# Two attentions on one core: half pairs of exponentials for VectorE, memory and B's first segment asked sooner

## The chip, the cores and the metric

One core of a Trainium2 chip. Its engines run their own instruction streams beside each other: TensorE (PE, with the weight loads PEld shown apart), VectorE (DVE), ScalarE (ACT), GpSimd (POOL) and SyncE (SP), which here issues nearly all DMAs. The metric is the device time of one execution in microseconds (us); lower is better.

## The reference

Two independent attentions over 2048 tokens of width 576 with 32 heads of 18, all float32; their outputs are concatenated.

```python
# A: one key and one value head for all query heads
q = heads(x @ wq); k = x @ wk; v = x @ wv
p = softmax(einsum("bhqd,bkd->bhqk", q, k) * Dh ** -0.5)
a = merge(einsum("bhqk,bkd->bhqd", p, v)) @ wo
# B: four segments of 512, causal inside a segment, and a running memory
for s in range(4):
    logits = einsum("bhqd,bhkd->bhqk", qs, ks) * scale + mask
    a_dot = einsum("bhqk,bhkd->bhqd", softmax(logits), vs)
    a_mem = einsum("bhld,bhde->bhle", phi(qs), M) / (einsum("bhld,bhd->bhl", phi(qs), z)[..., None] + 1e-6)
    o = g * a_mem + (1.0 - g) * a_dot
    M = M + einsum("bhld,bhle->bhde", phi(ks), vs); z = z + einsum("bhld->bhd", phi(ks))
b = merge(o) @ wo
```

## The kernel before, in words

The first part (L156 to L606, up to about 290 us) projects q, k and v of A and B, splits them into float32r parts, stores them to DRAM, and sums B's memory. The attention stage follows, and its order on PE, ACT and DVE is written out by hand (L1086).

Its work is cut into blocks. A block of A, `("A", c, hg)`, is one chunk of 512 queries and four heads (two "pairs" of heads, `pr` 0 and 1) against 16 key tiles `kt` of 128: 32 items. A block of B, `("B", s, hg)`, is one segment and four heads against three key tiles: 6 items. There are 32 of each. `after` (L869) says behind which block of A each pair of B blocks runs; the pair shares one stack of operands. `its` lists the items, `turns` cuts each block into turns of three items, with one turn of two (the last one) in a block of A: 11 turns of A, 2 of B. `prods` does the same for the products, with its short turn at another place (`cut`).

The loop at L1110 makes one turn k:

- `scores` (L905) for the items of turn k: two matmuls for a pair into `E`, a PSUM tile of two banks, one bank per head; there are three such tiles. Then exponentials on ACT into `P`. The second item of a turn (`copied`) is first copied by DVE from `E` to `W` in SBUF, so that its PSUM tile comes free before ACT has reached it; ACT does it last.
- One step of B's memory (`ask_memory`, L809, from turn `ASK` on and only where the turn is all of A), or, when that has ended, one step of an output projection (`run_fill`, L856; 60 steps a projection, eight projections in all, two of which are done in the tail).
- One step of `slow`: pairs named in `BY_DVE` have their exponential computed by VectorE from bit operations and a polynomial (`exponentials`, L890, seven operations, into the tile `PD`). The first reads PSUM in the pair's own turn, the six others follow one a turn. Their products come late in the block, at the place that `LATE` gives.
- `products` (L949) for turn k-2: P times V into `O`. With the last products of a block, DVE copies `O` out and SP stores it.
- `due`: steps put down for later, which normalize finished heads (`finish`).

Operands come by DMA on SP in program order: `load_stackB` (L688) loads queries, bounds and keys of eight heads of B into `stB`, of which there are two buffers (16 issues a stack); `load_stackA` does the same for A; `load_vseg` loads a segment's values (one buffer); `load_qf` and `ask_memory` load what the memory step needs, for two segments, into `o` and `woA`. `prefetch` asks for the stack after the one in use. L997 to L1003 set the order at the start.

The tail, from L1141, ends the projection that has begun and does the last two with PE alone (L1163).

Of the kernel before, what the change touches and what calls it, by code (L numbers as in the profile page):

```python
# [8 lines left out]
F32 = mybir.dt.float32  # L9
# [3 lines left out]
U32 = mybir.dt.uint32  # L13
AF = mybir.ActivationFunctionType
# [14 lines left out]
SCALE = DH ** -0.5  # L29
# [3 lines left out]
PBUFS = 9  # L33
# [18 lines left out]
POLY = [1.0925606709321247, 32.334180715292455, 88.7610992882796, 4291.093056129828]  # L52
MANTISSA, ONE_BITS, EXPONENT = 0x7FFFFF, 0x3F800000, 0xFF800000

BY_DVE = ((0, 1),)
LATE = (12,)
QALL = [(slice(0, 36, 2), 0), (slice(1, 36, 2), 1), (slice(36, 54), 0)]
CA = 618
MZ = 126 + 32

LATE_ASK, ASK = (1, 2), 20


def below(rows, r0):
# [10 lines left out]
def attention_pair_kernel(ctx, tc, a_xT, a_w, a_wo, b_xT, b_w, b_wo, b_beta, ident_d, hmask_d, bmask_d, cmask_d, sel_d, zmask_d, selx_d, sely_d, out):  # L75
    nc = tc.nc
# [727 lines left out]
    def load_qf(s):  # L804
        qfs[s] = pa.tile([128, 5, C], F32, name="o", bufs=2)
        nc.sync.dma_start(qfs[s][:126, :4], qfB[s][:126, :4])
        nc.sync.dma_start(qfs[s][: RT[4], 4], qfB[s][: RT[4], 4])
# [47 lines left out]

    def run_fill():  # L856

        while fill:
            key, steps = fill[0]
            if next(steps, None) is not None:  # L860
                begun.add(key)
                filled[0] += 1
                return
            fill.pop(0)


    blocksA = [("A", c, hg) for c in range(NCH) for hg in range(8)]
    blocksB = [[("B", s, 2 * h8), ("B", s, 2 * h8 + 1)] for s in range(NSEG) for h8 in range(4)]
    after = [0, 0, 1, 1, 2, 3, 3, 4, 8, 9, 10, 12, 16, 17, 18, 20]  # L869
    blocks = []  # L870
    for n, b in enumerate(blocksA):
        blocks.append(b)
# [14 lines left out]

    slow, now = [], [0]

    def exponentials(p, e):  # L890

        y, u, w = p.bitcast(U32), pp.tile([128, 2, 512], F32, name="n", bufs=1), pp.tile([128, 2, 512], F32, name="q", bufs=1)
        v, stt = nc.vector, nc.vector.scalar_tensor_tensor
        v.tensor_scalar(y, e, EXP_A, EXP_B, op0=ALU.mult, op1=ALU.add)
        steps = [
            lambda: v.tensor_scalar(u.bitcast(U32), y, MANTISSA, ONE_BITS, op0=ALU.bitwise_and, op1=ALU.bitwise_or),
            lambda: v.tensor_scalar(w.bitcast(U32), y, EXPONENT, None, op0=ALU.bitwise_and),
            lambda: stt(p, u, POLY[0], u, op0=ALU.add, op1=ALU.mult),
            lambda: stt(p, p, POLY[1], u, op0=ALU.add, op1=ALU.mult),
            lambda: stt(p, p, POLY[2], p, op0=ALU.add, op1=ALU.mult),  # L900
            lambda: stt(p, p, POLY[3], w, op0=ALU.add, op1=ALU.mult),
        ]
        slow.extend((now[0] + 2 + i, p, step) for i, step in enumerate(steps))

    def scores(it, pr, copied):  # L905

        ab, c, hg, kt = it
        st = stacks[ab, c, hg // 2]
        h = 2 * (hg % 2) + pr
        e = psE.tile([128, 2, 512], F32, name="E")  # L910
        dve = ab == "A" and (kt, pr) in BY_DVE
        p = pp.tile([128, 2, 512], F32, name="PD" if dve else "P", bufs=1 if dve else PBUFS)
        state[it, pr] = p
        n = 512 if ab == "A" else 512 - 128 * kt if kt < 2 else 384
        if ab == "A":
            for j, r0 in enumerate(HALF):
                rows = slice(r0, r0 + KR)
                nc.tensor.matmul(e[:, j], kstA[rows, 128 * kt : 128 * kt + 128], st[rows, h, :], start=True, stop=True)  # L918
            if (kt, pr) in BY_DVE:
                exponentials(p, e)  # L920
                return lambda: None
        else:
            for k, c0 in BKEYS[kt]:
                ks = slice(128 * k, 128 * k + 128)
                for j, r0 in enumerate(HALF):
                    rows = slice(r0, r0 + KR)
                    nc.tensor.matmul(  # L927
                        e[:, j, c0 : c0 + 512 - 128 * k], st[rows, 4 + h, ks], st[rows, h, 128 * k :], start=True, stop=True
                    )
        src = e  # L930
        if copied:
            src = pp.tile([128, 2, 512], F32, name="W", bufs=2)
            nc.vector.tensor_copy(src[:, :, :n], e[:, :, :n])  # L933

        def exponential():
            nc.scalar.activation(p[:, :, :n], src[:, :, :n], AF.Exp, scale=SCALE)  # L936
            if ab == "B":

                m = len(BKEYS[kt])
                diag = p.rearrange("p a (b t) -> p a b t", t=256)[:, :, 0:m, 0:128]  # L940
                nc.gpsimd.affine_select(  # L941
                    diag, diag, pattern=[[0, 2], [0, m], [1, 128]], base=0, channel_multiplier=-1, compare_op=ALU.is_ge, fill=0.0
                )

        return exponential
# [3 lines left out]
    def products(b, m, hf):  # L949


        ab, c, hg = b
        if m == hf == 0:
            acc[0] = psO.tile([128, C], F32, name="O")
        o = acc[0]
        last = (NKT - 1 if ab == "A" else 2) == m
        for j in range(4):
            kt = turn_of[j // 2][m] if ab == "A" else m
            p = state[b + (kt,), j // 2]
            assert all(x[1] is not p for x in slow)  # L960
            k, p0, q0, n = (kt, 256 * hf, 256 * hf, 256) if ab == "A" else BHALF[kt][hf]
            if ab == "A":
                v = VA[:, VW * kt : VW * kt + 32]
            else:
                v = vseg[c][:, k, VW * (4 * hg + j) : VW * (4 * hg + j) + 32]
            nc.tensor.matmul(  # L966
                o[32 * j : 32 * j + 32, q0 : q0 + n],
                v,
                p[:, j % 2, p0 : p0 + n],
                start=m == hf == 0,  # L970
                stop=last and hf == 1,
            )
        if last and hf:
            osb = pa.tile([128, C], F32, name="oe", bufs=4)
            nc.vector.tensor_copy(osb, o)  # L975
            od = oA if ab == "A" else oB
            nc.sync.dma_start(od[c][4 * hg : 4 * hg + 4].rearrange("h r t -> (h r) t"), osb)
            return hg
        return None
# [12 lines left out]
    def prefetch(ab, upto):  # L992
        for k in keys[ab][:upto]:
            if k not in stacks:
                stacks[k] = (load_stackA if ab == "A" else load_stackB)(*k[1:])

    prefetch("B", 1)  # L997
    load_vseg(0)
    prefetch("B", 2)
    load_qf(1)  # L1000
    memory = ask_memory()
    next(memory)
    prefetch("A", 2)  # L1003
    FILL = 60
    later, weighed, loaded, summing = [], {}, [0], set()
# [80 lines left out]
    with tc.manual_schedule(engines={ENG.PE, ENG.Activation, ENG.DVE}):  # L1086
# [3 lines left out]
        for n, b in enumerate(blocks):  # L1090
            ms = [m for m in range(len(its)) if block_of[m] == n]
            items = [(m, k) for m in ms for k in range(2)]
            for out_, cut in ((turns, len(items) // 3), (prods, len(items) // 3 - 2)):
                at_ = split(len(items), cut)
                out_ += [items[a:z] for a, z in zip(at_, at_[1:])]
        at(ASK + 4, 0, lambda: True, lambda k: load_qf(2))
# [13 lines left out]
        for k in range(len(turns) + 2):  # L1110
            now[0] = k
            exps = [scores(its[n], pr, i == 1) for i, (n, pr) in enumerate(turns[k])] if k < len(turns) else []
            for i in (0, 2, 1) if len(exps) == 3 else range(len(exps)):
                exps[i]()
            if memory is None:
                run_fill()
            elif k >= ASK and all(its[n][0] == "A" for n, pr in turns[k]) and next(memory, None) is None:
                memory = None

            ends = k > 1 and any(hf and its[n][3] == (NKT - 1 if its[n][0] == "A" else 2) for n, hf in prods[k - 2])  # L1120
            if slow and (slow[0][0] <= k or not ends):
                slow.pop(0)[2]()
            for n, hf in prods[k - 2] if k > 1 else []:
                ab, c = its[n][:2]
                hg = products(its[n][:3], its[n][3], hf)
                if hg in (6, 7):
                    finish(k, ab, c, hg)
                if hg == 7 and ab == "B" and c + 1 < NSEG:
                    load_vseg(c + 1)
            due(k)  # L1130
            if k == len(turns):
                halve_w(0)
            for n, pr in turns[k] if k < len(turns) else []:
                it = its[n]
                ab = it[0]
                if pr == 0:
                    prefetch(ab, keys[ab].index((ab, it[1], it[2] // 2)) + 2)
                    if it in (("A", 0, 2, 8), ("A", 0, 5, 8)):
                        load_wo(*(("B", b_wo) if it[2] == 2 else ("A", a_wo)))

        while fill and fill[0][0] in begun:  # L1141
            due(k, 4)
            run_fill()
            if filled[0] % FILL == 0:
                fill.pop(0)
            k += 1

        rows = [key for key, steps in fill] + [blocks[-1][:2]]
# [113 lines left out]
```

## Time and profile before

| | us |
|---|---|
| median of 3 runs | 1418.96 (1418.83 to 1419.97) |
| profiled execution | 1422.47, its span 1420.7 |
| PE busy | 1404.0 (99%) |
| ACT busy | 1205.4 (85%) |
| DVE busy | 964.4 (68%) |
| POOL busy | 244.6 (17%) |
| ACT, exponentials from PSUM (L936, P<-E) | 800 of them, 780.8 busy |
| ACT, exponentials from SBUF (L936, P<-W) | 384 of them, 426.3 busy |
| DVE, copies W (L933) | 384 of them, 461.2 busy |

Busy times are the union of an engine's instructions. Instructions of one engine overlap in the records, so the time that one costs is read from its start to the start of the next, not from its length. A busy PE is not a PE at its limit. In the timeline rows a bracket gives the idle time before a row and what ended it; SPq rows are issues of DMAs, with no landing time.

### The profile page before, as it was taken

To read this page: it belongs to the slowest core of one execution; us is meant where nothing else is said; L and a number is where in the kernel's file an instruction comes from. 1 tells how busy PE (TensorE), PEld (TensorE's weight loads), DVE (VectorE), ACT (ScalarE), POOL (GpSimd) and SP (SyncE) were. 2 spreads that over 40 slices of the span, in tenths; PEclk is the share of its full clock that TensorE was granted. 3 is DMA by queue.
4 is the path that set the end of the run, shared out by engine and by line. 5 is a ranking of instruction groups with operands and counts; after the bars stand their busy time and mean duration, and the time that the engine had idled before them with its cause. 6 is when DMAs were issued, how large, how long until landed. Compare 5 with 4: busy or idle time off the path is not lost.

```text
span 1420.7 us, 39951 instructions
## 1 busy us (share of the span) xinstructions
PE 1404.0 (99%) x17132; PEld 843.3 (59%) x17132; DVE 964.4 (68%) x1157; ACT 1205.4 (85%) x1447; POOL 244.6 (17%) x326
## 2 busy tenths in 40 slices
PE   9999999999999999999999999999999999999998
PEld 6788888745555555555555555555555555555558
DVE  6656456456677767776766777666767766777663
ACT  4543434479999999999999999999999999999991
POOL 2431000003313213221110160131011400100002
PEclk9999999999999999999999999999999999999999
DMA  9766546557564535332312543232104221110013
GB/s 283 253 216 188 166 146 214 174 171 214 156 214 159 165 120 166 91 109 77 110 58 70 166 128 92 62 107 80 51 34 132 67 76 44 60 45 18 9 59 112
DMA packets 90720, 172.63 MB, mean 122 GB/s; under 512 B 14576, under 2 KB 22889, under 8 KB 90110
## 3 DMA queue, kind: packets, MB, share of 16 engines
q1 hardware_dynamic: 84122, 160.01, 36.0%
q0 software_dynamic: 1664, 4.78, 1.3%
q10 hardware_dynamic: 4752, 5.24, 1.1%
q8 instruction: 135, 2.21, 0.7%
q14 instruction: 47, 0.39, 0.1%
HBM read 99.32 MB, written 70.67 MB: 120 GB/s over the span
## 4 chain that ended last, share of the span: by engine, by line
PE 68%; ACT 7%; issue 2%; DMA 1%; DVE 1%; SPq 0%; ACTq 0%; DVEq 0%
PE O L966 31%; PE E L918 20%; PE F L773 11%; ACT P L936 7%; PE E L927 3%; PE E L1163 2%; PE F L829 1%; DMA stB<-qB 0%; DVE W L933 0%; PE F L1163 0%; PE O L1163 0%; DMA oA<-oe 0%; DMA stB<-kB 0%; DMA sm<-oA 0%; SPq L696 0%
## 5 line engine op out<-in xcount | busy, mean ns | idle before, releaser
L936 ACT ACTIVATE P<-E 128x1024 f32<-128x1024 f32 (+1 forms) x800 | 780.8, 1059 | 12.7 <-PE E L918 12.3
L933 DVE COPY W<-E 128x1024 f32<-128x1024 f32 (+1 forms) x384 | 461.2, 1201 | 248.8 <-PE E L918 189.2
L966 PE MATMUL O<-P,VA 128*32 128x256 f32 x7936 | 508.8, 380 | 0.0
L936 ACT ACTIVATE P<-W 128x1024 f32<-128x1024 f32 (+1 forms) x384 | 426.3, 1110 | 3.4 <-DVE W L933 3.2
L966 PEld LDWEIGHTS O<-P,VA 128*32 128x32 f32 x7936 | 262.2, 110 | 147.6 <-issue 6.6
L918 PE MATMUL E<-stA,kstA 56*128 56x512 f32 x1920 | 329.4, 439 | 1.8 <-DVE W L933 1.1
L918 PEld LDWEIGHTS E<-stA,kstA 56*128 56x128 f32 x1920 | 154.7, 184 | 178.2 <-ACT P L936 113.7
L941 POOL TENSOR_SCALAR_AFFINE_SELECT P<-P 128x256 f32<-128x256 f32 (+1 forms) x192 | 95.0, 495 | 480.3 <-ACT P L936 446.9
L761 POOL TENSOR_TENSOR o<-o,rb 126x512 f32<-126x512 f32 (+1 forms) x55 | 79.9, 1468 | 408.9 <-DMA o<-oA 146.0
L773 PE MATMUL F<-woB,o 126*32 126x192 f32 (+1 forms) x1920 | 127.4, 338 | 0.3 <-DVE osb L797 0.3
L966 PE MATMUL O<-P,vseg 128*32 128x256 f32 (+2 forms) x1536 | 81.8, 344 | 0.8 <-issue 0.8
L773 PEld LDWEIGHTS F<-woB,o 126*32 126x32 f32 (+1 forms) x1920 | 38.2, 108 | 70.6 <-issue 63.6
L975 DVE COPY oe<-O 128x512 f32<-128x512 f32 x64 | 44.3, 692 | 41.8 <-PE O L966 41.0
L252 PE MATMUL pj<-xh,wBl 128*126 128x512 f32 x180 | 72.4, 403 | 0.0
L252 PE MATMUL pj<-xh,wBh 128*126 128x512 f32 x180 | 71.9, 400 | 0.0
L121 ACT CAST qp<-pj 126x512 fp32r<-126x512 f32 (+1 forms) x54 | 31.0, 585 | 46.1 <-DVE kmB L450 32.4
L966 PEld LDWEIGHTS O<-P,vseg 128*32 128x32 f32 x1536 | 49.1, 109 | 25.4 <-issue 2.9
L773 PE MATMUL F<-woA,o 126*32 126x192 f32 (+1 forms) x960 | 63.9, 338 | 0.0
L927 PE MATMUL E<-stB 56*128 56x256 f32 (+3 forms) x512 | 61.3, 347 | 1.4 <-ACT P L936 0.9
L122 DVE TENSOR_TENSOR qp<-pj,qp 126x512 fp32r<-126x512 f32 (+1 forms) x54 | 36.7, 685 | 35.6 <-ACT qp L121 35.3
L252 PE MATMUL pj<-xl,wBh 128*126 128x512 f32 x144 | 57.3, 399 | 0.0
L927 PEld LDWEIGHTS E<-stB 56*128 56x128 f32 x512 | 38.6, 185 | 31.1 <-ACT P L936 20.8
(194 smaller groups left out, 1387.8 us busy)
## 6 DMA issues: line engine op xcount, KB each, us to landing
stB<-kB SPq DMA_DIRECT2D x96, 144.0 KB
stB<-qB SPq DMA_DIRECT2D x32, 288.0 KB
stA<-qA SPq DMA_DIRECT2D x30, 288.0 KB
oA<-oe SPq DMA_DIRECT2D x32, 256.0 KB
oB<-oe SPq DMA_DIRECT2D x32, 256.0 KB
qA<-qp SPq DMA_DIRECT2D x16, 504.0 KB
kB<-qp SPq DMA_DIRECT2D x16, 504.0 KB
qB<-qp SPq DMA_DIRECT2D x16, 504.0 KB
```

The costliest lines, as they stand in the source:

```text
L121: hold(nc.scalar.copy(qp[:R, 0, :n], src))
L122: hold(nc.vector.tensor_tensor(qp[:R, 1, :n], src, qp[:R, 0, :n].bitcast(F32), op=ALU.subtract))
L252: nc.tensor.matmul(dst, w[:, c0 : c0 + M], x, start=i == 0, stop=i == len(ops) - 1)
L761: return lambda: tc.keep_in_program_order(nc.gpsimd.tensor_tensor(dst, a, b, op=op))
L773: nc.tensor.matmul(dst[32 * j : 32 * j + 32], parts[ab, c][: RT[t], t, r0 : r0 + 32], wo[ab][: RT[t], t, c0 : c0 + n], start=start, stop=stop,
L918: nc.tensor.matmul(e[:, j], kstA[rows, 128 * kt : 128 * kt + 128], st[rows, h, :], start=True, stop=True)
L927: nc.tensor.matmul(e[:, j, c0 : c0 + 512 - 128 * k], st[rows, 4 + h, ks], st[rows, h, 128 * k :], start=True, stop=True)
L933: nc.vector.tensor_copy(src[:, :, :n], e[:, :, :n])
L936: nc.scalar.activation(p[:, :, :n], src[:, :, :n], AF.Exp, scale=SCALE)
L941: nc.gpsimd.affine_select(diag, diag, pattern=[[0, 2], [0, m], [1, 128]], base=0, channel_multiplier=-1, compare_op=ALU.is_ge, fill=0.0)
L966: nc.tensor.matmul(o[32 * j : 32 * j + 32, q0 : q0 + n], v, p[:, j % 2, p0 : p0 + n], start=m == hf == 0, stop=last and hf == 1,)
L975: nc.vector.tensor_copy(osb, o)
```

## The change

- `BY_DVE` names pairs (0, 1) and (5, 0) of each block of A instead of (0, 1). `exponentials` now takes one head of a pair, 512 columns; ACT does the other head, from `W`, of which DVE copies that half. `PD` gets two buffers. The six operations after the first come two a turn over three turns. `LATE` puts the products of these pairs at places 7 and 12.
- `ASK` goes from 20 to 6, and with it the second `load_qf` from turn 24 to 10. The first `load_qf` and the load of `mz` (`ask_memory`) stand on SP ahead of the first stack of B.
- `after`: B's first segment (four stacks) runs behind the first block of A. Before, it was two stacks behind the first and two behind the second. The second segment is two stacks behind the third block and two behind the fourth; before, one, two and one behind the third to fifth.
- The short turn of the products moves one turn on.
- `run_fill` drops a projection with its sixtieth step and begins no seventh in the loop. As built, the first projection step stands behind the third block of A (before: within the fourth), and all 360 stand before the last turns of the last block; before, three of them stand behind the last products.

```diff
-BY_DVE = ((0, 1),)
-LATE = (12,)
+BY_DVE = ((0, 1), (5, 0))
+LATE = (7, 12)
...
-LATE_ASK, ASK = (1, 2), 20
+LATE_ASK, ASK = (1, 2), 6
...
-        while fill:
+        if fill and filled[0] < 6 * FILL:
             key, steps = fill[0]
-            if next(steps, None) is not None:
-                begun.add(key)
-                filled[0] += 1
-                return
-            fill.pop(0)
+            next(steps)
+            begun.add(key)
+            filled[0] += 1
+            if filled[0] % FILL == 0:
+                begun.remove(key)
+                fill.pop(0)
...
-    after = [0, 0, 1, 1, 2, 3, 3, 4, 8, 9, 10, 12, 16, 17, 18, 20]
+    after = [0, 0, 0, 0, 2, 2, 3, 3, 8, 9, 10, 12, 16, 17, 18, 20]
...
-    def exponentials(p, e):
+    def exponentials(p, e, whole):
 
-        y, u, w = p.bitcast(U32), pp.tile([128, 2, 512], F32, name="n", bufs=1), pp.tile([128, 2, 512], F32, name="q", bufs=1)
-        v, stt = nc.vector, nc.vector.scalar_tensor_tensor
+        u, w = (pp.tile([128, 512], F32, name=nm, bufs=1) for nm in "nq")
+        v, stt, y = nc.vector, nc.vector.scalar_tensor_tensor, p.bitcast(U32)
...
-        slow.extend((now[0] + 2 + i, p, step) for i, step in enumerate(steps))
+        slow.extend((now[0] + 2 + i, p, ops[2 * i : 2 * i + 2], whole) for i in range(3))
...
-        p = pp.tile([128, 2, 512], F32, name="PD" if dve else "P", bufs=1 if dve else PBUFS)
+        p = pp.tile([128, 2, 512], F32, name="PD" if dve else "P", bufs=2 if dve else PBUFS)
...
-            if (kt, pr) in BY_DVE:
-                exponentials(p, e)
-                return lambda: None
+            if dve:
+                exponentials(p[:, 0], e[:, 0], p)
...
-        src = e
+        src, hs = e, slice(0, 2)
         if copied:
             src = pp.tile([128, 2, 512], F32, name="W", bufs=2)
-            nc.vector.tensor_copy(src[:, :, :n], e[:, :, :n])
+            hs = slice(1, 2) if dve else slice(0, 2)
+            nc.vector.tensor_copy(src[:, hs, :n], e[:, hs, :n])
 
         def exponential():
-            nc.scalar.activation(p[:, :, :n], src[:, :, :n], AF.Exp, scale=SCALE)
+            nc.scalar.activation(p[:, hs, :n], src[:, hs, :n], AF.Exp, scale=SCALE)
...
+    load_qf(1)
+    memory = ask_memory()
+    next(memory)
     prefetch("B", 1)
     load_vseg(0)
     prefetch("B", 2)
-    load_qf(1)
-    memory = ask_memory()
-    next(memory)
     prefetch("A", 2)
...
-            for out_, cut in ((turns, len(items) // 3), (prods, len(items) // 3 - 2)):
+            for out_, cut in ((turns, len(items) // 3), (prods, len(items) // 3 - 1)):
...
             if slow and (slow[0][0] <= k or not ends):
-                slow.pop(0)[2]()
+                for op in slow.pop(0)[2]:
+                    op()
...
             run_fill()
-            if filled[0] % FILL == 0:
-                fill.pop(0)
             k += 1
```

More of the change, by code (lines that the diff above doesn't have):

```diff
@@ L888, in attention_pair_kernel @@
     slow, now = [], [0]
-    def exponentials(p, e):
-        y, u, w = p.bitcast(U32), pp.tile([128, 2, 512], F32, name="n", bufs=1), pp.tile([128, 2, 512], F32, name="q", bufs=1)
-        v, stt = nc.vector, nc.vector.scalar_tensor_tensor
+    def exponentials(p, e, whole):
+        u, w = (pp.tile([128, 512], F32, name=nm, bufs=1) for nm in "nq")
+        v, stt, y = nc.vector, nc.vector.scalar_tensor_tensor, p.bitcast(U32)
         v.tensor_scalar(y, e, EXP_A, EXP_B, op0=ALU.mult, op1=ALU.add)
-        steps = [
+        ops = [
             lambda: v.tensor_scalar(u.bitcast(U32), y, MANTISSA, ONE_BITS, op0=ALU.bitwise_and, op1=ALU.bitwise_or),
@@ L959, in products @@
             p = state[b + (kt,), j // 2]
-            assert all(x[1] is not p for x in slow)
+            assert all(x[3] is not p for x in slow)
             k, p0, q0, n = (kt, 256 * hf, 256 * hf, 256) if ab == "A" else BHALF[kt][hf]
```

## The prediction

> **What bounds the kernel now.** I read the page's busy times first, then a table of windows over single blocks of A, then the timeline of one block turn by turn, then the timeline of SP, which issues all loads of the attention stage. I call a trip of the loop at L1110 a turn: three pairs of scores, three products of the turn two before, sometimes a step of a projection.
>
> One block of A late in the run; columns are window, length, then busy time and count of PE, PEld, DVE, ACT, POOL, then granted clock, DMA share, GB/s:
>
> ```profile
> 1291.20:1320.20 29.00, 29.00 (x410) 15.16 (x408) 20.51 (x21) 28.77 (x32) 0.00 (x0) 1.00 0.06 21
> ```
>
> A block takes 29.0 us. PE and ACT both look full, so busy time decides nothing; the steps between starts do. The start of the last block (columns: start, length, engine, line, operation; idle before it and what ended that):
>
> ```profile
> 1346.14 0.72 PE L918 MATMUL E<-stA,kstA 56*128 56x512 f32 x4
> ...
> 1348.12 1.19 PE L918 MATMUL E<-stA,kstA 56*128 56x512 f32 x6
> ...
> 1349.21 2.10 ACT L936 ACTIVATE P<-E 128x1024 f32<-128x1024 f32 x2
> ...
> 1351.00 0.95 PE L918 MATMUL E<-stA,kstA 56*128 56x512 f32 x6
> 1351.54 1.94 ACT L936 ACTIVATE P<-E 128x1024 f32<-128x1024 f32 x2 [0.23 <-PE E L918]
> ...
> 1353.36 1.06 ACT L936 ACTIVATE P<-W 128x1024 f32<-128x1024 f32 x1
> 1353.64 0.97 PE L918 MATMUL E<-stA,kstA 56*128 56x512 f32 x6
> 1353.78 0.69 DVE L975 COPY oe<-O 128x512 f32<-128x512 f32 x1 [0.72 <-PE O L966]
> 1354.31 1.95 ACT L936 ACTIVATE P<-E 128x1024 f32<-128x1024 f32 x2
> ...
> 1356.12 1.08 ACT L936 ACTIVATE P<-W 128x1024 f32<-128x1024 f32 x1
> 1356.30 0.96 PE L918 MATMUL E<-stA,kstA 56*128 56x512 f32 x6
> ...
> 1358.28 1.22 DVE L898 SCALAR_TENSOR_TENSOR PD<-n 128x1024 f32<-128x1024 f32 x1
> ```
>
> ACT, from start to start: a W exponential 0.95 (1353.36 to 1354.31), two from E 1.81 (1354.31 to 1356.12), so 2.76 a full turn. PE: 2.65 a turn (1351.00, 1353.64, 1356.30). ACT is the slower one by 0.1 a turn. But in the first turn of a block VectorE takes pair (0, 1) whole, and ACT has 1.81 us of work against more than 2.65 of PE: from 1349.21 two exponentials last to 1351.02, the next starts at 1351.54. ACT loses 0.52 in every block, 31 exponentials for 28.47 plus 0.52 is the 29.0. That is the bound, with one hole a block.
>
> **The change part by part. The split pairs.** (0, 1) and (5, 0) go half to VectorE, half to ACT, from W, because both stand second in their turn. What does an ACT instruction of half the size cost? The trace has three quarters of it (W of 1024, then two E and one W of 768; the start of each to the next):
>
> ```profile
> 381.17 1.13 ACT L936 ACTIVATE P<-W 128x1024 f32<-128x1024 f32 x1
> 382.11 1.58 ACT L936 ACTIVATE P<-E 128x768 f32<-128x768 f32 x2
> 383.50 0.93 ACT L936 ACTIVATE P<-W 128x768 f32<-128x768 f32 x1
> 384.23 1.81 ACT L936 ACTIVATE P<-E 128x1024 f32<-128x1024 f32 x2
> ```
>
> W costs 0.94 at 1024 and 0.73 at 768, so 0.52 at 512. ACT's work per block: 28.47 minus one whole exponential (0.95) plus two halves (1.04) is 28.56. The turn with a half has 1.81+0.52 = 2.33. PE's first turn of a block gets shorter too: the products' short turn moves one on, out of the turn with two score pairs (1346.14 to 1348.12, 1.98 us) into this one. A score pair is 0.23 (0.95 for six matmuls, 0.72 for four), so the two products left out there are worth 2.65-0.23-1.98 = 0.44; after, the last turn is 2.42 and the first 2.21, the block's sum on PE stays 9x2.65+2.42+2.21 = 28.48. ACT's 2.33 against 2.21: the hole closes. In the turn of (5, 0) ACT's 2.33 stands against 2.65, which three turns' lead of 0.1 each just covers. So a block goes towards 28.56, at most 0.44 faster; PE's 28.48 leaves hardly any reserve, so I take 0.38, and 31 blocks give 12 us (the first is discussed below). Bounds: -4 (only the extra 0.09 to 0.12 a block, if the hole moves instead of closing) to +14; other holes of ACT in blocks that end a segment might close as well, which I put at another 4 at most.
>
> VectorE pays for it: 7 operations of 1024 become 14 of 512. The copy of 128x512 at 0.69 bounds a half from above, half of 1.22 from below; a turn with a copy W (1.22) and two halves has 2.44 to 2.60, under 2.65. Hidden, with up to 0.2 to spare; where a reciprocal falls into such a turn, W comes late as it does now. The Trainium skill, "VectorE: DVE Perf Modes", section on the TRN2 errata, says that a fixed latency is paid for each instruction, so that small tiles pay it once for each; that speaks against halves. Its fp32 formula would make the two halves 1.38 instead of 1.22, an estimate from that page; the 1.22 at 1024 agrees with it. Even so the turn stays below PE's.
>
> **The loads in front of B.** This is the part that I think decides. All loads stand in one order on SP. Sizes, and SP's rows of before around the first segment of B:
>
> ```profile
> stB<-kB SPq DMA_DIRECT2D x96, 144.0 KB
> stB<-qB SPq DMA_DIRECT2D x32, 288.0 KB
> ...
> o<-qfB SPq DMA_DIRECT2D x2, 1008.0 KB
> ...
> woA<-mzB SPq DMA_DIRECT2D x1, 790.0 KB
> ```
> ```profile
> 294.65 0.37 SPq L141 DMA_DIRECT2D stA<-qA  x1
> 295.39 0.32 SPq L141 DMA_DIRECT2D stB<-qB  x1
> ...
> 299.01 3.38 SPq L696 DMA_DIRECT2D stB<-kB  x3
> ...
> 307.30 0.40 SPq L883 DMA_DIRECT2D vseg<-vB  x1
> 307.75 0.46 SPq L141 DMA_DIRECT2D stB<-qB  x1
> ...
> 310.35 6.44 SPq L151 DMA_DIRECT2D stB<-shB  x4
> ...
> 322.32 0.25 SPq L697 DMA_DIRECT2D stB<-ones_d  x1
> 322.61 0.31 SPq L806 DMA_DIRECT2D o<-qfB  x1
> ...
> 333.48 0.35 SPq L977 DMA_DIRECT2D oA<-oe  x1
> ...
> 336.54 0.33 SPq L141 DMA_DIRECT2D stB<-qB  x1
> ```
> ```profile
> 350.77 0.64 SPq L806 DMA_DIRECT2D o<-qfB  x1
> ...
> 367.41 0.25 SPq L697 DMA_DIRECT2D stB<-ones_d  x1
> ...
> 379.72 0.34 SPq L141 DMA_DIRECT2D stB<-qB  x1
> ...
> 390.04 0.26 SPq L697 DMA_DIRECT2D stB<-ones_d  x1
> ```
>
> An issue waits until the eighth before it has landed: the ninth row after 294.65 is the one at 299.01, so that first load took 4.4 us, and the big o<-qfB of 322.61 holds the eighth behind it until 333.48. A stack of B is some 1.7 MB in 15 or 16 issues: 11.6 us from 295.39 to 307, 14.6 with vseg in between (307.75 to 322.32), 10.3 at the quickest (379.72 to 390.04). ACT needs a stack for 9.3 us:
>
> ```profile
> 321.87 1.83 ACT L936 ACTIVATE P<-E 128x1024 f32<-128x1024 f32 x2
> ...
> 331.19 1.90 ACT L936 ACTIVATE P<-E 128x1024 f32<-128x1024 f32 x2
> ```
>
> stB has two buffers. Before, two stacks run, then a block of A of 29 us in which the next two are fetched. After, all four run behind the first block of A, and the queue has o<-qfB and woA<-mzB (1.9 MB) ahead of the first, and the second o<-qfB between the second and third. Step by step:
> - o<-qfB and woA<-mzB took from the landing of the stack before them, 322.32+4.4 = 326.7, to 336.54, where SP goes on: 9 to 10 us. By that all behind them moves, 9.3 say. Stack 0 is in at 307+9.3+4.4 = 321, just when it is wanted. Stack 1 is issued to 331.6, in at 336; ACT, some 0.7 later, starts at 336.7 instead of 331.2: 5.5 lost, and its work ends at 346.
> - Then the rest of stA (4 us of issues), denB, o<-qfB at about 336.6. From such an issue to the last of the stack behind it: 350.77 to 367.41, 16.6; with two stores of O in between 17.6. Stack 2 is issued to 354.2, in at 358.6, ACT at 359.3: 13.3 lost, until 368.6.
> - Stack 3's buffer is free since 346; its issues run from 355 to 365.5 at the quickest pace, in at 370, ACT at 370.7: 2 lost.
>
> Together 21 us in which ACT and PE stand still, in the first segment of B. Bounds: 13 if each stack comes at the quickest pace and the 1.9 MB are gone in 8; 27 if stack 3 takes 14.6. What is gained or lost in the first block of A (the memory's steps, which may themselves wait a little for woA, included) disappears into this wait. The later segments run two stacks after a block of A, like now, and are loaded in time.
>
> **Memory and projection steps.** 24 steps of memory move from turns 20 on to turns 6 on, their matmuls and copies are the same: 0 net, within 1. Projection steps begin one block sooner and are done some turns before the end; they run beside ACT either way. The gain is in the tail:
>
> ```profile
> 1381.79 1.16 PE L773 MATMUL F<-woB,o 126*32 126x192 f32 x24
> 1382.06 0.69 DVE L975 COPY oe<-O 128x512 f32<-128x512 f32 x1 [1.23 <-PE O L966]
> ...
> 1384.03 2.53 PE L1163 MATMUL E<-stB,P 126*128 126x288 f32 x17 [0.75 <-DVE P L1100]
> ```
>
> Without the last steps and their copies, the halves that L1163 waits for follow 0.7 after oe, and the last products start about a microsecond sooner: 2 us, bounds 0 and 3.5.
>
> **Sum.** +21 for the waits, -12 for the blocks, -2 for the tail: 7 us slower. The profiled execution had a span of 1420.7 and took 1422.5, a little over the runs' median of 1418.96; the difference is applied to the median: 1426.
>
> **The rivals.**
> 1. Loads keep up. If the stacks come as fast as they are used, only the gains are left: 1419-14 = 1405. It decides where a stack with its neighbours in the queue takes under some 9.3 us; for a mere draw the lost 21 must fall to 14. Against it: no stack of before came in under 10.3, and most took 11.6 or more. For it: the rows of before never show how fast a stack would come with ACT waiting. The Trainium skill, "DMA: Bandwidth & Descriptors", section Specifications, gives about 358 GB/s from HBM for a core; a stack would take 5 us by that, an estimate from that page, and nothing would wait. 14%.
> 2. The waits come, the smoothing doesn't: PE's 28.48 and VectorE's late copies keep a block at 29.0, the extra instruction is paid for. 21 and no 12: 1438. For it: the reserve is below 0.1 a block. Against it: PE's block is no longer than now, and the copies now end in time beside operations of 1.22. 16%.
> 3. Less waiting (15), more gain (all of 14, tail 3, some other holes): 1416 to 1419, no change or a little faster. 18%.
>
> **How the numbers follow.** The forecast, +7, has 52%, its own range 1420 to 1433 from the bounds of the waits with the middle gain. About 0.2% (2.8 us) is what a measurement here can tell. Faster: rival 1 and a third of rival 3, 0.20. Same: half of rival 3 and the low edge of the forecast, 0.11. Slower: 0.69. The range, 1411 to 1437, leaves out most of rival 1 and half of rival 2.
>
> **What would show it.** Three stretches of idle ACT between 330 and 372, before the second, third and fourth stack of B, PE waiting for DMA stB, the second wait the longest (10 us or more); SP held at L151 behind o<-qfB just before it. Blocks of A late in the run at 28.6, without the 0.23 gap at their second turn. The first L1163 about 2 us sooner after the last exponential. I am wrong if stacks 2 and 3 land without a wait, or if late blocks of A stay at 29.0.

## The result, and the profile after

| us | before | after |
|---|---|---|
| median of 4 runs each | 1419.47 (1418.83 to 1420.25) | 1438.74 (1437.05 to 1440.4) |
| profiled execution | 1422.47 | 1440.4 |
| its span | 1420.7 | 1438.6 |
| first exponential at | 292.3 | 291.8 |
| 32 blocks of A | 935.0 | 936.5 |
| B, first segment (8 blocks) | 37.9 | 56.4 |
| B, other segments (24 blocks) | 114.3 | 114.6 |
| last exponential's end to the end | 41.3 | 39.3 |

The ratio is 1.0134, 95% interval 1.0119 to 1.0149: the change makes the kernel 19 us slower. The lower rows of the table add up to the spans; they are read from the starts of the exponentials, a block being the time from its first one to the first one of the next block. The two spans differ by 17.9 us: B's first segment takes 18.5 longer, the blocks of A lose 1.5 instead of gaining, the tail gives 2 back. In the rows of the changed kernel the line numbers of the attention stage are one higher than before (its exponentials are L937, not L936).

**B's first segment.** The timeline of ACT after the change, rows with a wait in front, while the four stacks run:

```profile
333.46 1.73 ACT L937 ACTIVATE P<-E 128x1024 f32<-128x1024 f32 x2 [2.88 <-PE E L927]
...
355.66 1.73 ACT L937 ACTIVATE P<-E 128x1024 f32<-128x1024 f32 x2 [11.65 <-PE E L927]
...
359.53 1.56 ACT L937 ACTIVATE P<-E 128x768 f32<-128x768 f32 x2 [1.12 <-PE E L927]
...
368.13 1.72 ACT L937 ACTIVATE P<-E 128x1024 f32<-128x1024 f32 x2 [1.17 <-PE E L927]
```

ACT stands before the second, third and fourth stack, and names as releaser the scores L927, which themselves need the stack. With one of 0.95 at 337.07, inside the second stack, the waits sum to 17.8 of the 18.5. The two inside the stacks (0.95 and 1.12) stand right behind the long ones. There TensorE's granted clock was lower, 0.76 from 333 to 340 and 0.58 from 355 to 362, against 1.00 from 325 to 333 and from 362 on; 24 products of B took 2.57 at 356.24 and 1.40 at 362.55. The timeline of SP shows why the third stack is the worst:

```profile
332.29 0.33 SPq L806 DMA_DIRECT2D o<-qfB  x1
...
333.67 0.34 SPq L978 DMA_DIRECT2D oA<-oe  x1
335.41 0.34 SPq L978 DMA_DIRECT2D oB<-oe  x1
336.76 0.34 SPq L141 DMA_DIRECT2D stB<-qB  x1
...
341.67 2.08 SPq L151 DMA_DIRECT2D stB<-shB  x4
...
350.51 0.25 SPq L697 DMA_DIRECT2D stB<-ones_d  x1
```

The first issue of the third stack is at 336.76, behind o<-qfB and two stores, its last at 350.51, and ACT starts on it at 355.66: 18.9 us from first issue to use, while a stack keeps ACT busy for 9.3.

**A quiet block of A.** ACT at the start of the block that runs from 1312.37 to 1341.12, then the table of windows for that block:

```profile
1312.37 2.12 ACT L937 ACTIVATE P<-E 128x1024 f32<-128x1024 f32 x2
1314.18 0.83 ACT L937 ACTIVATE PD<-W 128x512 f32<-128x512 f32 x1
1314.70 2.13 ACT L937 ACTIVATE P<-E 128x1024 f32<-128x1024 f32 x2
```
```profile
1312.37:1341.12 28.75, 28.75 (x412) 15.18 (x408) 21.49 (x29) 28.75 (x33) 0.00 (x0) 1.00 0.03 12
```

From start to start two exponentials take 1.81 and a half one 0.52, 2.33 for the turn, and no wait of ACT is left in the block, where 0.23 stood before. The block takes 28.75 instead of 29.0. Counted over the run, 22 blocks are shorter than before, by 7.7 together, and ten are longer, by 9.2.

**A block of A that got longer.** The block from 408.37 to 440.91 took 32.54, before 29.82. ACT, VectorE and GpSimd in the middle of it:

```profile
428.76 1.06 ACT L937 ACTIVATE P<-W 128x1024 f32<-128x1024 f32 x1 [2.17 <-DVE W L934]
```
```profile
424.25 1.56 DVE L899 SCALAR_TENSOR_TENSOR PD<-n 128x512 f32<-128x512 f32 x1
425.85 1.75 DVE L900 SCALAR_TENSOR_TENSOR PD<-PD,n 128x512 f32<-128x512 f32 x1
427.52 1.21 DVE L934 COPY W<-E 128x1024 f32<-128x1024 f32 x1
```
```profile
423.98 1.29 POOL L761 TENSOR_TENSOR o<-o,rb 126x512 f32<-126x512 f32 x1 [0.29 <-DMA rb<-rB]
425.77 1.28 POOL L761 TENSOR_TENSOR o<-o,rb 126x512 f32<-126x512 f32 x1 [0.50 <-DMA rb<-rB]
```

ACT waits 2.17 for the copy W. In front of that copy stand the two operations of a half, and they took 1.56 and 1.75, each beside one of GpSimd's multiplications L761, the normalization of a finished chunk. The copy, which reads PSUM, took its usual 1.21. Late copies W cost ACT 3.2 us over the whole run before and 11.5 after, the last number of these rows of the two pages:

```profile
L936 ACT ACTIVATE P<-W 128x1024 f32<-128x1024 f32 (+1 forms) x384 | 426.3, 1110 | 3.4 <-DVE W L933 3.2
```
```profile
L937 ACT ACTIVATE P<-W 128x1024 f32<-128x1024 f32 (+1 forms) x352 | 403.2, 1145 | 12.2 <-DVE W L934 11.5
```

How long VectorE's operations are on the average is in the table of groups of VectorE by shape (count, busy, mean ns), here for the changed kernel:

```profile
L900 DVE SCALAR_TENSOR_TENSOR PD<-PD,n 128x512 f32<-128x512 f32 x64 | 49.2, 769 | 2.2
L902 DVE SCALAR_TENSOR_TENSOR PD<-PD,q 128x512 f32<-128x512 f32 x64 | 47.3, 739 | 2.2
L899 DVE SCALAR_TENSOR_TENSOR PD<-n 128x512 f32<-128x512 f32 x64 | 45.2, 707 | 0.0
L901 DVE SCALAR_TENSOR_TENSOR PD<-PD 128x512 f32<-128x512 f32 x64 | 45.2, 707 | 0.0
...
L898 DVE TENSOR_SCALAR q<-PD 128x512 uint32<-128x512 uint32 x64 | 33.4, 521 | 0.0
...
L897 DVE TENSOR_SCALAR n<-PD 128x512 uint32<-128x512 uint32 x64 | 30.5, 476 | 0.0
```

The six rows sum to 250.8 us. What they would be without GpSimd beside them is shown by an experiment below. The trace has 23 of these operations that took over 0.3 longer than the median of their kind. Each of them began after a TENSOR_TENSOR of GpSimd that was still running, and ended 0.28 (L897, L898) or 0.55 (L899 to L902) after that one's end, so it stood until GpSimd was done.

### The profile page after: what moved, and what is told of

Read it like the earlier page. It is cut to its first block, busy times and chain, and to the rows that moved or that the text cites. A ratio compares the mean times of both kernels' runs of the same rounds, so it can differ in the third digit from the quotient of the medians.

```text
span 1438.6 us, 40386 instructions
## 1 busy us (share of the span) xinstructions
PE 1403.5 (98%) x17132; PEld 846.1 (59%) x17132; DVE 995.6 (69%) x1413; ACT 1207.8 (84%) x1479; POOL 236.6 (16%) x326
## 4 chain that ended last, share of the span: by engine, by line
PE 68%; DMA 4%; DVE 4%; issue 2%; ACT 1%; SPq 1%; POOL 0%; DVEq 0%; POOLq 0%; ACTq 0%
PE O L967 31%; PE E L919 20%; PE F L773 11%; PE E L927 3%; DVE W L934 2%; PE E L1163 2%; DMA stB<-qB 2%; DMA stB<-shB 1%; ACT P L937 1%; DMA o<-qfB 1%; PE F L829 1%; DMA stB<-kB 1%; SPq L696 1%; DVE PD L901 0%; DVE sm L729 0%
## 5 line engine op out<-in xcount | busy, mean ns | idle before, releaser
L937 ACT ACTIVATE P<-E 128x1024 f32<-128x1024 f32 (+1 forms) x800 | 797.1, 1097 | 21.5 <-PE E L927 18.1
L934 DVE COPY W<-E 128x1024 f32<-128x1024 f32 (+2 forms) x416 | 465.2, 1119 | 224.9 <-PE E L919 148.5
L937 ACT ACTIVATE P<-W 128x1024 f32<-128x1024 f32 (+1 forms) x352 | 403.2, 1145 | 12.2 <-DVE W L934 11.5
L919 PE MATMUL E<-stA,kstA 56*128 56x512 f32 x1920 | 323.8, 435 | 6.7 <-DVE W L934 5.7
L761 POOL TENSOR_TENSOR o<-o,rb 126x512 f32<-126x512 f32 (+1 forms) x55 | 75.2, 1379 | 474.3 <-DMA rb<-rA 191.4
L927 PE MATMUL E<-stB 56*128 56x256 f32 (+3 forms) x512 | 63.2, 352 | 16.1 <-DMA stB<-kB 8.7
L967 PE MATMUL O<-PD,VA 128*32 128x256 f32 x512 | 72.3, 381 | 0.0
L927 PEld LDWEIGHTS E<-stB 56*128 56x128 f32 x512 | 40.1, 190 | 44.9 <-ACT P L937 23.6
L895 DVE TENSOR_SCALAR PD<-E 128x512 uint32<-128x512 f32 x64 | 44.2, 690 | 28.9 <-PE E L919 28.0
```

The source lines that it names most:

```text
L761: return lambda: tc.keep_in_program_order(nc.gpsimd.tensor_tensor(dst, a, b, op=op))
L927: nc.tensor.matmul(e[:, j, c0 : c0 + 512 - 128 * k], st[rows, 4 + h, ks], st[rows, h, 128 * k :], start=True, stop=True)
L934: nc.vector.tensor_copy(src[:, hs, :n], e[:, hs, :n])
L937: nc.scalar.activation(p[:, hs, :n], src[:, hs, :n], AF.Exp, scale=SCALE)
L967: nc.tensor.matmul(o[32 * j : 32 * j + 32, q0 : q0 + n], v, p[:, j % 2, p0 : p0 + n], start=m == hf == 0, stop=last and hf == 1,)
```

## The experiments

The theory after this reading: two losses that add up. (a) Four stacks in a row through two buffers and one queue cost about 18 us, with or without the split. (b) The split is worth 0.25 to 0.43 in a quiet block, but its operations on VectorE now meet L761 about twice as often as before, and each meeting holds one up by as much as a microsecond, which ends as a late W on ACT. Rivals: the loads put in front of B, not the four stacks, make the waits; the memory steps, not L761, make VectorE late.

### e1_split: the split alone

```diff
-LATE_ASK, ASK = (1, 2), 6
+LATE_ASK, ASK = (1, 2), 20
-    after = [0, 0, 0, 0, 2, 2, 3, 3, 8,
+    after = [0, 0, 1, 1, 2, 3, 3, 4, 8,
```

and the loads at the start in the order of before; all else as changed.

> The split of the pairs alone, with the order of blocks, of the memory and of the first loads as before. Theory: quiet blocks of A fall from 29.0 to about 28.75, and from 29.16 to 28.73 behind B, which is 7 to 8 us over the run; VectorE's operations that meet GpSimd's L761 give some 4 us of it back, the tail stays: 1413 to 1417. Rival (the split is worth nothing, or costs in itself): 1418 to 1423.

Measured: 1425.18 against 1420.26, ratio 1.0038 (1.0023 to 1.0053), so slower, and outside both expectations. Its blocks of A sum to 937.6, 2.6 more than before, though its quiet ones take 28.7. Five blocks take 30.6 to 31.1. In one of them ACT waits 1.63 behind L902 at 1.66 instead of 0.69:

```profile
1249.46 1.06 ACT L937 ACTIVATE P<-W 128x1024 f32<-128x1024 f32 x1 [1.63 <-DVE W L934]
```
```profile
1246.62 1.66 DVE L902 SCALAR_TENSOR_TENSOR PD<-PD,q 128x512 f32<-128x512 f32 x1
```
```profile
1244.76 2.98 POOL L761 TENSOR_TENSOR o<-o,rb 126x512 f32<-126x512 f32 x2 [1.17 <-DMA o<-oA]
```

GpSimd runs two L761 from 1244.76 to 1247.74 there, over the start of L902. No memory step is near (they are long done at 1246), so the rival on the memory doesn't explain this block.

### e2_order: the order alone

```diff
-LATE_ASK, ASK = (1, 2), 20
+LATE_ASK, ASK = (1, 2), 6
-    after = [0, 0, 1, 1, 2, 3, 3, 4, 8,
+    after = [0, 0, 0, 0, 2, 2, 3, 3, 8,
```

in the kernel of before, with the loads and the projection steps of the changed one; VectorE takes whole pairs as before.

> The order alone (four stacks of B behind the first block of A, memory from turn 6, its loads in front, projection steps ending sooner), the pair (0, 1) whole on VectorE as before. Theory: the waits for stB, 18 to 19 us, are all there, the tail gives 2 back, blocks of A as before: 1434 to 1437. Rival (the early memory and the waits disturb more than the segment of B, or the split made the waits longer): outside 1432 to 1440, or the waits under 15 us.

Measured: 1437.87, ratio 1.0131 (1.0113 to 1.0148), a little over the theory's numbers. The order alone gives the whole loss; the split on top of it (1.0134) gives nothing. ACT in B's first segment:

```profile
336.28 1.73 ACT L937 ACTIVATE P<-E 128x1024 f32<-128x1024 f32 x2 [4.56 <-PE E L928]
...
356.14 1.73 ACT L937 ACTIVATE P<-E 128x1024 f32<-128x1024 f32 x2 [8.80 <-PE E L928]
```

The segment takes 55.2, against 56.4 in the changed kernel. Part of the wait moves from the third stack to the second; ACT's idle time in the segment is 16.6 in all, against 18.1.

### e3_two_two: two stacks behind the first block of A, two behind the second

```diff
-    after = [0, 0, 0, 0, 2, 2, 3, 3, 8,
+    after = [0, 0, 1, 1, 2, 2, 3, 3, 8,
```

> The changed kernel with B's first segment two stacks behind the first block of A and two behind the second. Theory: only the second stack waits (3 to 4 us, for the loads put in front), the 14 us in front of the third and fourth go: 1421 to 1425. Rival (the loads in front of B are the cause, not four stacks in a row): 1430 or more.

Measured: 1444.99, ratio 1.0177 (1.016 to 1.0194), a clear miss of the theory; the number is the rival's. The first segment fell to 42.3 as the theory wants, but the second went from 37.7 to 50.2. ACT and SP there:

```profile
444.09 1.73 ACT L937 ACTIVATE P<-E 128x1024 f32<-128x1024 f32 x2 [11.65 <-PE E L927]
```
```profile
421.86 1.53 SPq L748 DMA_DIRECT2D rb<-rB  x2
423.44 0.67 SPq L141 DMA_DIRECT2D stB<-qB  x1
...
439.38 0.25 SPq L697 DMA_DIRECT2D stB<-ones_d  x1
```

ACT waits for the second stack of the second segment. It is issued from 423.44 to 439.38, behind loads and stores that finish heads of the first segment (the two rb of 421.86 are the last in front of it), and ACT starts on it at 444.09. With this order the second segment begins at 422.9, in the middle of those loads; in the changed kernel at 440.9. So "four in a row" is too narrow a name for (a): what counts is what stands on the queue ahead of each stack, and here the wait went to the second segment, which begins 18 us sooner than in the changed kernel.

### e4_old_loads: four stacks in a row, the loads as before

```diff
-LATE_ASK, ASK = (1, 2), 6
+LATE_ASK, ASK = (1, 2), 20
-    load_qf(1)
-    memory = ask_memory()
-    next(memory)
     prefetch("B", 1)
     load_vseg(0)
     prefetch("B", 2)
+    load_qf(1)
+    memory = ask_memory()
+    next(memory)
```

> The changed kernel with the memory's loads behind the first two stacks and asked from turn 20, four stacks in a row kept. Theory: the third stack still finds its buffer only when the first is done and comes 10 us late or more, the fourth 3 to 5, the second not at all: 13 to 17 us of waits, 1432 to 1437. Rival (the loads in front are the cause): under 1427.

Measured: 1448.64, ratio 1.0195 (1.0178 to 1.0213), above what was expected. With o<-qfB and woA<-mzB behind the first two stacks, the second comes in time, but the third, which now has them in front of it, is later than in the changed kernel (13.19 against 11.65):

```profile
352.36 1.73 ACT L937 ACTIVATE P<-E 128x1024 f32<-128x1024 f32 x2 [13.19 <-PE E L927]
```

The first segment takes 53.6, and the second has a wait of 5.79 of its own (44.7 in all). So the place in front of B is not what makes the waits: with the loads moved the waits stay, and go to the third stack and to the second segment, which has no wait with the early loads (37.7). The loads themselves are not cleared by this, since they still stand ahead of the third stack (its first issue is at 335.35, when woA<-mzB has landed). No run has four stacks in a row with these loads out of their way, so the shares of the two stay open. The blocks of A were at 940.0, for which no run separates the causes.

### e5_after_pool16 and e6_before_pool16: L761 on 16 columns

```diff
-            return lambda: tc.keep_in_program_order(nc.gpsimd.tensor_tensor(dst, a, b, op=op))
+            return lambda: tc.keep_in_program_order(nc.gpsimd.tensor_tensor(dst[:, :16], a[:, :16], b[:, :16], op=op))
```

In the changed kernel and in the one before. The normalization of the other 496 columns of every chunk is left out, so GpSimd's instructions stay in number and place, but are short.

> The changed kernel with GpSimd's weighing products (L761) on 16 of 512 columns; this leaves out the normalization of the other columns, all waits and loads stay. Theory (VectorE's operations between SBUF tiles stand still while a long L761 runs, and halves meet it twice as often): the slow ones among L897 to L902 go, blocks of A with a late W fall to about 28.75 but for the reciprocals and the memory's block, 936.5 us of blocks become 922 to 926: 1424 to 1429. Rival (the late W come from the halves' own load on VectorE or from PE): no less than 1435.

> The kernel before with L761 on 16 of 512 columns, normalization left out as in the run beside it. Theory: whole operations of 1024 met L761 15 times and had slack for most of them: 1416 to 1419. Rival (L761 costs any kernel as much as it costs the split): 1408 or less.

Measured: after, 1432.34, ratio 1.0089 (1.0071 to 1.0107); before, 1420.51, ratio 1.0007 (0.9997 to 1.0016). The changed kernel gets some 6 us from it, less than expected; the one before nothing that can be told, so the expected 1416 to 1419 missed too. The groups of VectorE in the changed kernel with the short L761:

```profile
L900 DVE SCALAR_TENSOR_TENSOR PD<-PD,n 128x512 f32<-128x512 f32 x64 | 44.3, 692 | 2.2
...
L897 DVE TENSOR_SCALAR n<-PD 128x512 uint32<-128x512 uint32 x64 | 26.7, 417 | 0.0
```

The six groups sum to 229.4, so L761 adds 21.4 us to VectorE's work in the changed kernel. The same view gives 210.9 and 199.6 for the two kernels with whole pairs, so 11.3 before. Halving the operations about doubled what the meetings cost. Before, this had room: late copies W cost ACT 3.2 us, and 1.7 with the short L761. In the changed kernel they fell from 11.5 to 6.3, and its blocks of A to 928.4, short of the expected 922 to 926. Six blocks that the change had made longer:

| block (chunk, head group) | before | after | after, L761 on 16 columns |
|---|---|---|---|
| (0, 1) | 29.16 | 30.90 | 30.93 |
| (0, 2) | 29.82 | 32.54 | 29.06 |
| (0, 5) | 29.87 | 31.49 | 28.59 |
| (1, 6) | 29.35 | 29.93 | 28.60 |
| (2, 6) | 29.02 | 30.10 | 28.60 |
| (3, 2) | 29.00 | 29.79 | 28.73 |

Of these only (0, 1) keeps its loss. There GpSimd multiplies nothing. In the changed kernel ACT and VectorE show, in that block:

```profile
400.00 1.06 ACT L937 ACTIVATE P<-W 128x1024 f32<-128x1024 f32 x1 [1.98 <-DVE W L934]
```
```profile
394.61 0.74 DVE L834 TENSOR_SCALAR o<-F,gt 72x512 f32<-72x512 f32 x1
395.38 0.70 DVE L838 TENSOR_SCALAR rb<-F 32x512 f32<-32x512 f32 x1
...
397.44 0.95 DVE L729 RECIPROCAL sm<-sm 112x128 f32<-112x128 f32 x1
398.43 0.29 DVE L732 TENSOR_SCALAR sm<-sm,omg 112x128 f32<-112x128 f32 x1
398.74 2.35 DVE L934 COPY W<-E 128x1024 f32<-128x1024 f32 x2
```

Two copies of the memory step, two operations of a half (in the rows left out) and a reciprocal stand in front of W. That is the rival on the memory, and it is right for this one block; the order alone shows it too, with 30.66 there.

### e7_split_pool16 and e8_split_pieces: the split alone, L761 short or cut

e7 is the split alone with L761 on 16 columns, as above, the rest of the normalization left out. e8 is the split alone with the whole multiplication in four pieces:

```diff
-            return lambda: tc.keep_in_program_order(nc.gpsimd.tensor_tensor(dst, a, b, op=op))
+            def run():
+                for i in range(4):
+                    cs = slice(128 * i, 128 * i + 128)
+                    tc.keep_in_program_order(nc.gpsimd.tensor_tensor(dst[:, cs], a[:, cs], b[:, cs], op=op))
+
+            return run
```

> The split alone with L761 on 16 of 512 columns, normalization left out. Theory: with the meetings gone the split is worth what the quiet blocks show: 1409 to 1414. Rival (the split is worth nothing by itself): 1420 or more.

> The split alone, L761 complete but cut into four pieces of 128 columns. Theory (VectorE waits for the end of the instruction of GpSimd that it meets, not for a share of a port): an operation of VectorE waits 0.4 us instead of 1.1, most of the late W go: 1412 to 1418. Rival (the two share the port's rate, or the pieces follow each other without a gap): 1423 or more.

Measured: e7 1413.88, ratio 0.996 (0.9945 to 0.9974); e8 1415.67, ratio 0.9968 (0.9957 to 0.9979). Both fell where the theory put them. The split that costs 5 us with L761 in one piece gains 4 to 6 with L761 short or cut. The kernel before gained nothing that can be told from the short L761 (e6), so the gain is the split's; the pieces were not run in the kernel before. The operations of the halves sum to 229.4 in e7 and 241.1 in e8, against 252.1 in e1; the blocks of A to 926.1, 928.5 and 937.6. e8 computes the whole and is the fastest of the complete kernels here, 0.3% under the one before.

### e9_after_pieces: the changed kernel with the four pieces

> The changed kernel, with each multiplication of a finished chunk on GpSimd (L761) cut into four pieces of 128 columns. Theory: the loss has two parts that add up, the waits of B's first segment for its stacks (18 us, not touched by the pieces) and the blocks of A in which VectorE's halves meet GpSimd. The split alone went from 1425.2 to 1415.7 with the pieces, 9.5 us less; here the blocks of A fall from 936.5 to 927-930, B's first segment stays at 55-57, and the time is 1429 to 1433. Rival: the blocks with memory steps, not the meetings, are what the early memory costs; then the time stays at 1435 or more.

Measured: 1437.12 against 1421.27, ratio 1.0101 (1.0084 to 1.0118). In microseconds that is the rival's number; as a ratio it lies below the 1.0134 of the changed kernel, with intervals that do not overlap. The blocks of A came to 932.1, not 927 to 930. Where the rest went is seen in VectorE, GpSimd and ACT in block (0, 6):

```profile
567.03 3.06 DVE L902 TENSOR_SCALAR n<-PD 128x512 uint32<-128x512 uint32 x1
570.02 0.41 DVE L903 TENSOR_SCALAR q<-PD 128x512 uint32<-128x512 uint32 x1
```
```profile
563.10 3.37 POOL L764 TENSOR_TENSOR o<-o,rb 126x128 f32<-126x128 f32 x8
566.43 1.71 POOL L764 TENSOR_TENSOR rb<-rb 72x128 f32<-72x128 f32 x4
568.10 1.71 POOL L764 TENSOR_TENSOR o<-o,rb 72x128 f32<-72x128 f32 x4
```
```profile
571.60 1.06 ACT L942 ACTIVATE P<-W 128x1024 f32<-128x1024 f32 x1 [1.71 <-DVE W L939]
```

Several multiplications stand one behind the other on GpSimd, and L902 (L897 without the added lines), 0.41 by itself, took until 570.09, when their row ends at 569.81. Here the pieces let nobody in. Three blocks of e9 have such an operation (3.06, 2.5 and 2.2 us), one block of e8. These three blocks are together 3.9 longer than in e5, about the whole difference of 932.1 to 928.4. It is not the rule inside a row of pieces: near the start of the same row another L902 took its usual time.

```profile
548.32 0.42 DVE L902 TENSOR_SCALAR n<-PD 128x512 uint32<-128x512 uint32 x1
```
```profile
547.55 3.77 POOL L764 TENSOR_TENSOR o<-o,rb 126x128 f32<-126x128 f32 x8 [4.21 <-DMA rb<-rB]
```

Of the fourteen L902 of e9 that overlap pieces, eleven took at most 0.67. The three long ones all began beside pieces of 72 partitions, but two of the eleven did too, so the cause stays open. (0, 1), the memory's block, stayed at 30.89.

## Why the prediction came out as it did

It had the sign, but 7 us where 19 were measured, outside its range of 1411 to 1437. Two of its three terms came out near their size, the waits (18.5 for 21) and the tail (2); the blocks of A did not.

- **The bound, and the hole of 0.52.** Right: the turn with a half takes 2.33 as worked out, the hole is gone, and a quiet block takes 28.75. That is above the 28.56 of ACT's own work, but 0.25 to 0.43 under before; 0.38 was taken.
- **"VectorE pays for it ... Hidden, with up to 0.2 to spare."** This is the step that failed, and with it the term "31 blocks give 12 us": measured, the blocks lost 1.5. The working took the price of a half from rows in which GpSimd stood still. Beside L761 a half took up to 1.1 longer, the copy W came late, and ACT waited for it. With L761 short (e5) the blocks gain 6.6 against before: 26 of them gain 10.4, close to the 0.38 each that was taken, and six lose 3.8. So 8.1 of the missing 13.5 are the meetings; of the rest, as e5 shows it, 1.8 is block (0, 1) and 1.0 the last block, for whose loss no run shows a cause. In e1 this step alone turns the expected gain into a loss of 5 us, and e7 and e8 give the gain back when only L761 is changed. The Trainium skill, "SBUF — State Buffer", section "Who interferes with whom", states the rule that would have warned: a VectorE instruction with two inputs in SBUF contends with a GpSimd instruction that reads SBUF, one in a mode that uses both ports contends with GpSimd as well, and whichever issues second blocks until the first is done. The trace agrees on which operations are hit: L899 and L900 at 1.56 and 1.75 beside L761 against 0.68 and 0.69 alone, while none of the 37 copies W of 128x1024 that overlap a TENSOR_TENSOR of GpSimd took over 1.23. It agrees on the order too: the L900 of 425.85 began 0.08 after an L761 and ended 0.55 after that one's end. That it is a port lock is that page's word; the runs show the meeting and its price.
- **The loads in front of B, 21.** Right in size and in place: 18.5 in the first segment, three waits as named, the longest (11.65) before the third stack, predicted 13.3; before the second 2.88 instead of 5.5, before the fourth 1.17 instead of 2. SP was held at L151 behind o<-qfB, as named (the issue of 341.67 is the eighth behind the o<-qfB of 332.29). The sum was too large at its start: the loads in front moved the first stack's last issue by 5.0 (307.00 to 311.95), not by 9.3, and what follows came sooner by about that. From the second o<-qfB to the third stack's last issue it took 18.2 (332.29 to 350.51), 17.6 in the working. The 2.1 us of waits inside the stacks, at the lower granted clock, were not in the sum. (The 299.01 of the working is the eighth row behind 294.65, not the ninth, which is what its rule says.) The heading of that part was not right: e4 shows that the waits come as well when those loads stand behind two stacks. The working, which counted all that goes through the queue and the two buffers, was better than its heading.
- **Memory and projection, 0 within 1.** Too low for the block (0, 1), which lost 1.7; the early memory puts its copies beside a half and a reciprocal. With the order alone, (0, 1) and (0, 2) together lost 1.3.
- **The tail, 2.** Right: 41.3 became 39.3. The sign named for it holds as well: from the last exponential's end to the first L1163 it was 3.4 before, and 1.1 after. The first L1163 before is the one at 1382.88, not the row of 1384.03 that the working shows.

```profile
1378.34 1.14 ACT L936 ACTIVATE P<-W 128x1024 f32<-128x1024 f32 x1
...
1382.88 0.40 PE L1163 MATMUL E<-stB,P 126*128 126x288 f32 x1
```
```profile
1398.15 1.14 ACT L937 ACTIVATE P<-W 128x1024 f32<-128x1024 f32 x1
...
1400.42 0.40 PE L1163 MATMUL E<-stB,P 126*128 126x288 f32 x1
```

- **The rivals.** Number 2 gave the time, 1438, for another reason than it named: the smoothing came in every quiet block, and was eaten elsewhere. At 16% it was held too low, because the price of a late W was weighed only for a turn with a reciprocal in it.

## What to carry to other kernels

Before work is moved to VectorE, look at what GpSimd does at the same time and price the operation from rows in which both run; cutting it in halves about doubled what the meetings cost here (11.3 to 21.4 us). If the other engine's instruction can be cut, that may be worth more than the change itself: for the split alone it turned 5 us lost into 4 gained. And where stacks of operands go through two buffers and one queue, count all that goes through the queue against its pace over the whole stretch: in e3 and e4, moving stacks or loads from one place moved the wait to another.

## What the runs showed of the hardware

- A VectorE operation between SBUF tiles that runs beside GpSimd's TENSOR_TENSOR of 126x512 (1.29 us) took up to 1.1 longer, whole pairs and halves alike. A half ended 0.28 or 0.55 after GpSimd's instruction, as said above. So the halves paid about twice what whole pairs pay for the same number of elements (21.4 against 11.3 us). Copies and first steps that read PSUM kept their 0.69 and 1.22.
- With the pieces, the operations with two tensor inputs lost at most 0.3. Of the two with a single input, L902 was held up to the end of the row in three of fourteen meetings and lost at most 0.25 in the others; L903 never took over 0.69, 0.42 alone. The view of one tile in e9 (shortest, median and longest of 64, in ns) shows L902 and one of the others:

```profile
L902 DVE TENSOR_SCALAR n<-PD x64: 411/418/3065, 294.3 to 1379.9; 128x512 uint32<-128x512 uint32 x64
L904 DVE SCALAR_TENSOR_TENSOR PD<-n x64: 678/682/978, 296.2 to 1381.7; 128x512 f32<-128x512 f32 x64
```

Why L902 waits to the end of the row in those three was not tried.

- Behind the two long waits of TensorE in B's first segment the granted clock was 0.76 and 0.58, 1.00 elsewhere in that segment (windows of 3 to 8 us without such a wait), and 24 products took 2.57 instead of 1.40.
